# An attention, MLP and gated-convolution kernel: the residual u added by an accumulating store instead of by identity products

## The chip, the cores and the metric

The kernel runs on one core of a Trainium2 chip. The metric is the device time of one execution in microseconds; before the change three runs gave 1480.14, 1479.91 and 1478.4 us, median 1479.91.

The engines are named as in the profile: PE is TensorE (matmuls; PEld its weight loads), DVE is VectorE, ACT is ScalarE, POOL is GpSimd, and SP is SyncE, which issues DMAs.

## The reference

All arrays are float32. There are B = 8 batches of S = 576 tokens with D = 512 channels (8 heads of 64), so 4608 tokens.

```
scores = (q @ k.T) / 8, masked to block_i >= block_j (blocks of 64 tokens)
x  = softmax(scores) @ v                      # heads side by side: [8, 576, 512]
u  = x + (x.T @ U @ V).T                      # mixing over tokens, rank 32
z  = u + relu(u @ w_ch1) @ w_ch2              # MLP with 2048 hidden channels, residual u
gate = sigmoid(causal depthwise convolution of z, 5 taps)
out  = (gate * (z @ w_val)) @ w_out
```

The change concerns the line of z: how u is added to the MLP's result, and how the sum gets to DRAM, from where the gated stage reads it.

## The kernel before

Channels lie on partitions (four blocks d of 128), tokens along the free axis. The tokens of all batches form nine groups g of 512; a batch of 576 tokens is cut by the group boundaries into two pieces.

**Precision.** Every large product is made of three float32r products: each operand is split into a rounded part (names ending in h or hi) and the rest (l or lo), and hi·hi, hi·lo and lo·hi are added in PSUM. The rounded part is a copy on ACT (`hi_act`, L89), the rest a subtraction on POOL or DVE (`lo`, L95).

**Attention and mixing.** The attention of a pair of heads ends with x in a tile `xt` (five buffers), written by ACT out of PSUM (L605; the sums go to `lt`, L606) and multiplied on POOL by the reciprocal sums (L624). For the mixing it is transposed on PE (`mix_T`, L664, L672), multiplied with U (`mix_G`, L680), and in `mix_H` with V (L703); DVE adds the result into `xt` (L705), which then holds u, and ACT and POOL split it into the tiles uh and ul of its group. These tiles have two buffers, so pieces of a group that is too far ahead are put off (`later`) and done when the last step of an earlier group is out (`flush_later`); they come in a bunch around the change from one group to the next.

**The MLP.** For each group 16 steps f run over 128 hidden channels each. `emit_h1` makes 12 products (L833), ACT the rectified rounded part hh (L861) and DVE the rest hl (L862). `emit_o` makes 12 more with a block of W2 that SP loads from DRAM for each step into one of two buffers (L821), and adds them into four PSUM banks acc0 to acc3, one for each d (L885); for each d the order is hh, hl, hh. It runs one step behind `emit_h1`. In the first step of a group it first multiplies uh and ul with an identity matrix, for each d (L878): this puts u into acc. After the last step ACT copies acc to SBUF (L897), in tiles y with two buffers, and SP stores each of the four to `y_s` in DRAM (L898). Group 7's four copies go into tiles named gt, of which there are eight.

**Order of the work.** The order on PE is written out by hand: `gap()`, called twice in `emit_h1` and twice in `emit_o`, brings in the next pieces of the attention's stream at a fixed rate for each group. So around the change to a group PE runs: the last `emit_o` of the group before, `emit_h1` of steps 0 and 1 with pieces of attention between, then the first `emit_o`. All tiles of PSUM for attention and h come from four buffers with one tag. On the other engines and on SP a planner sets the order: it goes through the program with its own estimates of durations and gives each engine what is ready there by priority; the copies of acc, the tiles hh and hl and the additions into `xt` have a raised priority. Each engine then works through its list in that order, so an instruction that waits holds up everything behind it.

**After the MLP** (from 1268 us) `load_y` reads `y_s` back, DVE makes the gates, and PE the products with w_val (L975) and w_out (L999). The last group of `y_s` is read some rounds later than it is stored.

Of the kernel before, what the change touches and what calls it, by code (L numbers as in the profile page):

```python
# [9 lines left out]
F32R = mybir.dt.float32r  # L10
# [3 lines left out]
ALU = mybir.AluOpType  # L14
# [3 lines left out]
P = 128  # L18
# [4 lines left out]
def attn_moe_gate_kernel(ctx: ExitStack, tc: tile.TileContext, q, k, v, U, V, w1, w2, wval, convw, wout, out):  # L23
# [8 lines left out]
    ND = DM // P  # L32
    NF = DFF // P
# [52 lines left out]
    vec, act, pool, pe, sp = nc.vector, nc.scalar, nc.gpsimd, nc.tensor, nc.sync  # L86

    def hi_act(o, i):
        act.copy(o, i)  # L89
# [4 lines left out]
    def lo(eng, o, i, h):  # L94
        eng.tensor_tensor(o, i, f32(h), op=ALU.subtract)  # L95
# [51 lines left out]
    const = ctx.enter_context(tc.tile_pool(name="const", bufs=1, side="left"))  # L147
# [13 lines left out]
    def open_mlp_psum():  # L161
        first.close()
        psum["acc"] = mlp.enter_context(tc.tile_pool(name="accp", bufs=1, space=PSUM, side="left"))
# [38 lines left out]
    y_s = [dram.tile([P, ND, n], F32, name=f"y_s{g}") for g, (_, n) in enumerate(groups)]  # L202
# [15 lines left out]
    ident = ac_p.tile([P, P], F32, name="ident")  # L218
    make_identity(nc, ident)
    unit = const.tile([KC, KC], F32, name="unit")  # L220
    pool.tensor_copy(unit, ident[0:KC, 0:KC])
    identr = const.tile([P, P], F32R, name="identr")
    pool.tensor_copy(identr, ident)

    w1hi = w1_p.tile([P, ND, DFF], F32R, name="w1hi")
    w1lo = w1_p.tile([P, ND, DFF], F32R, name="w1lo")
# [400 lines left out]
    ut = {}  # L627
    gst = {}

    def u_tiles(g):  # L630
        if g not in ut:
            ut[g] = [u_p.tile([P, ND, GS], F32R, tag="u" + x, name="u" + x) for x in "hl"]
        return ut[g]


    def mix_pieces(b):
        t0, t1 = b * S, (b + 1) * S
        r = []
        for g, (a, n) in enumerate(groups):
            lo_t, hi_t = max(a, t0), min(a + n, t1)  # L640
            if lo_t < hi_t:
                r.append((g, lo_t - t0, hi_t - t0, lo_t - a))
        return r
# [3 lines left out]
    def mix_H2(pn):  # L647
        mix_H(pn, 0)
        yield
        mix_H(pn, 1)  # L650
# [39 lines left out]
    def mix_H(pn, i):  # L690
        pcs = mix_pieces(pn // NP)
        if i >= len(pcs):
            return
        gi, a0, a1, off = pcs[i]
        if gi >= 2 and gi > y_done[0] + 2:
            later.append((pn, i))
            return
        xt = xts[pn]
        d = pn % NP
        uh, ul = u_tiles(gi)  # L700
        w = a1 - a0
        ps = ps_p.tile([P, 512], F32, tag="a", name="pH")
        pe.matmul(ps[:, 0:w], gst[pn], vst[:, a0:a1], start=True, stop=True)  # L703
        with tc.high_priority():
            vec.tensor_tensor(xt[:, a0:a1], ps[:, 0:w], xt[:, a0:a1], op=ALU.add)  # L705
        hi_act(uh[:, d, off:off + w], xt[:, a0:a1])
        lo(pool, ul[:, d, off:off + w], xt[:, a0:a1], uh[:, d, off:off + w])

    def flush_later():
        if later and mix_pieces(later[0][0] // NP)[later[0][1]][0] <= y_done[0] + 2:  # L710
            mix_H(*later.pop(0))
# [113 lines left out]
    accs = {}  # L825
# [43 lines left out]
    def emit_o(s, gap):  # L869
        g, f = divmod(s, NF)  # L870
        t0, n = groups[g]
        if f == 0:
            if g == 0:
                open_mlp_psum()
            accs[g] = [psum["acc"].tile([P, GS], F32, tag=f"acc{d}", name=f"acc{d}") for d in range(ND)]
            for d in range(ND):
                for i, u in enumerate(ut[g]):
                    pe.matmul(accs[g][d][:, 0:n], identr, u[:, d, 0:n], start=(i == 0), stop=False)  # L878
        acc = accs[g]
        hh, hl = hts.pop(s)  # L880
        w = w2t.pop(s)
        for d in range(ND):
            ds = slice(d * P, (d + 1) * P)
            for i, (wi, x) in enumerate(((0, hh), (0, hl), (1, hh))):
                pe.matmul(acc[d][:, 0:n], w[:, wi, ds], x[:, 0:n], start=False, stop=(f == NF - 1 and i == 2))  # L885
            if d == 1:
                gap()
        gap()
        if f == NF - 1:
            ut.pop(g)  # L890
            for d in range(ND):
                if pbp and g < NG - 1:
                    y = pbp["g"].tile([P, GS + HALO], F32, tag="gt", name="gt")
                else:
                    y = late["y"].tile([P, GS], F32, tag="y", name="y")
                with tc.high_priority():
                    act.copy(y[:, 0:n], acc[d][:, 0:n])  # L897
                sp.dma_start(out=y_s[g][:, d, :], in_=y[:, 0:n])  # L898


    wv = {}
# [156 lines left out]
    def gap():  # L1058
        tick_count[0] += 1
        if tick_count[0] % EVERY == 0:  # L1060
            flush_later()
        pace[0] += pace[1]
        while pace[0] > 0 and pace[2] == 0:
            pace[0] -= 1.0
            r = next(stream, 2)
            if r:
                pace[2] = r
                if r == 2:
                    while later:
                        flush_later()  # L1070
                    open_pb()

    gated_conv[0] = GATE0
    for s in range(NS + LAG):
        g, f = divmod(s, NF)
# [5 lines left out]
        if f == 0 and g < B:  # L1081
            while g > 0 and not pace[2]:
                pace[0] = 1.0
                gap()
            if g > 0:
                emit_o(s - LAG, gap)
            if pace[2] != 2:
                pace[2] = 0
            aim(g)
        if s < NS:  # L1090
# [11 lines left out]
            if g == NG - 1 and 4 <= f < 4 + 2 * ND:  # L1102
                g_, d = divmod(f - 4, ND)
# [3 lines left out]
        if s >= LAG and not (f == 0 and g < B):  # L1107
            emit_o(s - LAG, gap)
# [54 lines left out]
```

## Time and profile before

| | |
|---|---|
| runs | 1480.14, 1479.91, 1478.4 us; median 1479.91 |
| profiled execution | span 1473.3 us; what lies around the span is the 6.6 us to the median of the runs |
| PE | 1426.3 us busy (97%), 6706 matmuls |
| DVE | 1054.8 us (72%) |
| ACT | 718.5 us (49%) |
| POOL | 297.8 us (20%) |
| DMA | 163.56 MB, all on SP's queue but for instructions |
| chain that ended last | PE 82%, DVE 10%, DMA 3%; line L878 in it 1% |

The span runs from the first to the last instruction; the profiled execution has no time of its own beside it, so its time is taken as span plus 6.6 us. A row of a timeline gives start, duration, engine, line, operation, tiles and shapes, the number of instructions merged into it, and in brackets the idle time before it with what ended it. Rows of a list of waits give the total in us, the number of waits and the longest. Matmuls overlap: their durations are longer than the distance between their starts.

### The profile page before, as it was taken

The page shows a single profiled execution, that of the slowest core. Times are in us where ns is not written, and L with a number is a line of the kernel's source. Part 1 is how long each engine was busy: PE and PEld are TensorE (multiplying, and loading weights), DVE is VectorE, ACT ScalarE, POOL GpSimd, SP SyncE. Part 2 cuts the span into 40 slices and gives each one's busy share as a digit, 9 for nine tenths or more (in the row PEclk, how much of TensorE's full clock was granted, in tenths as well). Part 3 has the DMA queues.
Part 4 walks back from the last instruction along what each step waited for, and adds up shares of the span by engine and source line. Part 5 has one row for each costly group of instructions (what it writes and reads, how often), then busy time and mean ns, then how long its engine had stood idle before and what let it go on. Part 6 is the DMA issues. An engine that isn't in the chain of part 4 may idle for free.

```text
span 1473.3 us, 20082 instructions
## 1 busy us (share of the span) xinstructions
PE 1426.3 (97%) x6706; PEld 1102.3 (75%) x6706; DVE 1054.8 (72%) x2224; ACT 718.5 (49%) x1529; POOL 297.8 (20%) x420
## 2 busy tenths in 40 slices
PE   6888899899999999999999999999999999999999
PEld 3656666677777777777777777777888888788887
DVE  7878877967786888777778878777224326399991
ACT  4676564555555546565555555555322221344332
POOL 2113332212121112112211211121122100343310
PEclk9999999999999999999999999999999999999999
DMA  6445764543343434333434433332255433223311
GB/s 123 104 106 154 217 210 130 152 110 96 84 102 110 95 96 111 96 86 82 124 82 111 114 83 96 96 95 70 86 159 167 147 128 123 92 72 101 109 56 65
DMA packets 246288, 163.56 MB, mean 111 GB/s; under 512 B 197669, under 2 KB 212261, under 8 KB 246186
## 3 DMA queue, kind: packets, MB, share of 16 engines
q1 hardware_dynamic: 246186, 162.29, 39.6%
q8 instruction: 53, 0.87, 0.3%
q14 instruction: 49, 0.40, 0.1%
HBM read 134.98 MB, written 27.26 MB: 110 GB/s over the span
## 4 chain that ended last, share of the span: by engine, by line
PE 82%; DVE 10%; DMA 3%; ACT 2%; issue 1%; SPq 1%; POOL 0%; DVEq 0%; ACTq 0%
PE acc L885 25%; PE h L833 25%; PE pPV L604 8%; PE o L999 7%; PE val L975 6%; PE pS L381 6%; DMA raw<-in_moe_w_ch_dram 1%; DVE wa L123 1%; DVE rq L425 1%; PE pG L680 1%; PE acc L878 1%; PE pS L416 1%; DVE wa L141 1%; PE pT L664 1%; DVE wa L120 1%
## 5 line engine op out<-in xcount | busy, mean ns | idle before, releaser
L885 PE MATMUL acc<-hh,w 128*128 128x512 f32 x1152 | 401.0, 402 | 0.0
L885 PEld LDWEIGHTS acc<-hh,w 128*128 128x128 f32 x1152 | 217.1, 188 | 67.6 <-issue 22.5
L833 PE MATMUL h<-uh,w1hi 128*128 128x512 f32 x576 | 238.5, 414 | 2.3 <-ACT lt L606 1.2
L833 PE MATMUL h<-uh,w1lo 128*128 128x512 f32 x576 | 226.4, 393 | 0.0
L885 PE MATMUL acc<-hl,w 128*128 128x512 f32 x576 | 225.9, 392 | 0.0
L833 PE MATMUL h<-ul,w1hi 128*128 128x512 f32 x576 | 225.7, 392 | 0.0
L862 DVE SCALAR_TENSOR_TENSOR hl<-h,hh 128x512 fp32r<-128x512 f32 x144 | 98.5, 684 | 143.2 <-ACT hh L861 142.0
L861 ACT ACTIVATE hh<-h 128x512 fp32r<-128x512 f32 x144 | 85.9, 596 | 173.9 <-PE h L833 167.9
L833 PEld LDWEIGHTS h<-uh,w1hi 128*128 128x128 f32 x576 | 108.6, 189 | 45.7 <-issue 20.4
L95 POOL TENSOR_TENSOR vlo<-vstk,vhi 128x320 fp32r<-128x320 f32 x46 | 43.0, 934 | 455.3 <-ACT vhi L89 389.2
L833 PEld LDWEIGHTS h<-uh,w1lo 128*128 128x128 f32 x576 | 108.4, 188 | 24.2
L885 PEld LDWEIGHTS acc<-hl,w 128*128 128x128 f32 x576 | 108.8, 189 | 19.8 <-issue 0.7
L833 PEld LDWEIGHTS h<-ul,w1hi 128*128 128x128 f32 x576 | 108.7, 189 | 19.6 <-issue 1.3
L957 DVE SCALAR_TENSOR_TENSOR gt<-yb,cw,gt 128x516 f32<-128x516 f32 (+1 forms) x144 | 115.2, 830 | 1.4
L381 PE MATMUL pS<-tq,tk 64*128 64x320 f32 (+4 forms) x576 | 96.7, 429 | 1.5 <-DVE hl L862 0.8
L95 POOL TENSOR_TENSOR yl<-yb,yh 128x512 fp32r<-128x512 f32 (+7 forms) x64 | 66.9, 1078 | 107.4 <-ACT yh L89 107.3
L386 ACT COPY s<-pS 128x320 f32<-128x320 f32 (+2 forms) x128 | 60.2, 497 | 48.7 <-PE pS L381 47.5
L95 POOL TENSOR_TENSOR ul<-xt,uh 128x512 fp32r<-128x512 f32 (+7 forms) x64 | 53.8, 850 | 108.0 <-ACT uh L89 107.9
L536 ACT ACTIVATE s<-s 128x448 f32<-128x448 f32 (+1 forms) x62 | 44.0, 710 | 64.8 <-DVE s L512 64.8
L381 PEld LDWEIGHTS pS<-tq,tk 64*128 64x128 f32 x576 | 43.8, 185 | 37.8 <-issue 22.2
L512 DVE TENSOR_TENSOR s<-s,mb 128x64 f32<-128x64 f32 (+4 forms) x160 | 68.7, 493 | 0.3
L605 ACT COPY xt<-pPV 64x128 f32<-64x128 f32 (+1 forms) x128 | 50.1, 391 | 25.8 <-PE pPV L604 23.9
(169 smaller groups left out, 2758.8 us busy)
## 6 DMA issues: line engine op xcount, KB each, us to landing
w<-w_s SPq DMA_DIRECT2D x144, 512.0 KB, 3.3
rawq<-in_q_dram SPq DMA_DIRECT2D x128, 72.0 KB, 2.8
rawk<-in_k_dram SPq DMA_DIRECT2D x128, 72.0 KB, 3.1
out_dram<-ot SPq DMA_DIRECT2D x35, 256.0 KB, 2.0
vstk<-in_v_dram SPq DMA_DIRECT2D x64, 128.0 KB, 2.7
raw<-in_moe_w_ch_dram SPq DMA_DIRECT2D x64, 128.0 KB, 2.8
raw<-in_moe_w_ch_dram SPq DMA_DIRECT2D x16, 512.0 KB, 3.9
w_s<-wo SPq DMA_DIRECT2D x16, 512.0 KB, 3.3
```

The lines of the kernel that those rows point to most:

```text
L95: eng.tensor_tensor(o, i, f32(h), op=ALU.subtract)
L381: pe.matmul(t[:, o:o + w], tk[me, kslice(j)], tq[me, a0:a1], start=True, stop=True)
L386: act.copy(stt[n][half_of[j]][:, d:d + o], t[:, 0:o])
L512: noted(3, vec.tensor_tensor(sv(n, j), sv(n, j), mb[:, q0[j]:], op=ALU.subtract))
L604: pe.matmul(o_, l_, r_, start=(i == 0), stop=(i == len(todo) - 1))
L833: pe.matmul(ps[:, 0:n], w[:, d, fs], x[:, d, 0:n], start=(d == 0 and i == 0), stop=(d == ND - 1 and i == 2))
L861: act.activation(hh[:, 0:n], ps[:, 0:n], AF.Relu)
L862: latest[0] = vec.scalar_tensor_tensor(hl[:, 0:n], ps[:, 0:n], 0.0, f32(hh[:, 0:n]), op0=ALU.max, op1=ALU.subtract)
L885: pe.matmul(acc[d][:, 0:n], w[:, wi, ds], x[:, 0:n], start=False, stop=(f == NF - 1 and i == 2))
L957: vec.scalar_tensor_tensor(gt[d][:, 0:gw], y[:, d, j:j + gw], cw[:, d, j:j + 1], gt[d][:, 0:gw], op0=ALU.mult, op1=ALU.add)
L975: pe.matmul(ps[:, 0:n], w[:, d, es], x[:, d, 0:n], start=(i == 0), stop=(i == 3 * ND - 1))
L999: pe.matmul(ps[:m, cs], x[:, e, a:a + m], w[:, e, cs], start=(i == 0), stop=(i == 3 * ND - 1))
```

## The change

`mix_H` gets a DMA from SP that writes each piece of u, as soon as it stands in `xt`, to the place in `y_s` where the MLP's result will go. The identity products are gone, and the first product with W2 of a group starts the accumulation in PSUM. The stores of the MLP's result are issued by POOL instead of SP, as DMAs that add to what lies in DRAM. The identity matrix in float32r isn't made any more.

```diff
@@ -219,8 +219,6 @@
     pool.tensor_copy(unit, ident[0:KC, 0:KC])
-    identr = const.tile([P, P], F32R, name="identr")
-    pool.tensor_copy(identr, ident)
@@ -703,6 +701,7 @@
         with tc.high_priority():
             vec.tensor_tensor(xt[:, a0:a1], ps[:, 0:w], xt[:, a0:a1], op=ALU.add)
+        sp.dma_start(out=y_s[gi][:, d, off:off + w], in_=xt[:, a0:a1])
         hi_act(uh[:, d, off:off + w], xt[:, a0:a1])
@@ -873,16 +872,13 @@
             accs[g] = [psum["acc"].tile([P, GS], F32, tag=f"acc{d}", name=f"acc{d}") for d in range(ND)]
-            for d in range(ND):
-                for i, u in enumerate(ut[g]):
-                    pe.matmul(accs[g][d][:, 0:n], identr, u[:, d, 0:n], start=(i == 0), stop=False)
         acc = accs[g]
...
             for i, (wi, x) in enumerate(((0, hh), (0, hl), (1, hh))):
-                pe.matmul(acc[d][:, 0:n], w[:, wi, ds], x[:, 0:n], start=False, stop=(f == NF - 1 and i == 2))
+                pe.matmul(acc[d][:, 0:n], w[:, wi, ds], x[:, 0:n], start=(f == 0 and i == 0), stop=(f == NF - 1 and i == 2))
@@ -895,7 +891,7 @@
                 with tc.high_priority():
                     act.copy(y[:, 0:n], acc[d][:, 0:n])
-                sp.dma_start(out=y_s[g][:, d, :], in_=y[:, 0:n])
+                pool.dma_start(out=y_s[g][:, d, :], in_=y[:, 0:n], accum_op=ALU.add)
```

## Rows read from the trace of the kernel before

**Rows 1.** Stretches: length, each engine's busy us (instructions), granted clock, DMA share, GB/s.

```profile
140.00:306.00 166.00, 152.35 (x684) 109.69 (x685) 135.76 (x280) 90.89 (x193) 47.45 (x53) 0.97 0.59 172
...
575.00:708.00 133.00, 133.00 (x658) 102.41 (x657) 104.67 (x233) 73.58 (x157) 24.31 (x44) 1.00 0.38 99
```

**Rows 2.** Waits of ACT: total us, times, longest us.

```profile
ACT y L897 <- DMA y_s<-y: 17.2, 9, 3.5
```

**Rows 3.** The identity products, line L878: durations in ns, first and last start.

```profile
L878 PE MATMUL acc<-uh,identr x36: 387/389/475, 140.1 to 1186.9; 128*128 128x512 f32 x36
...
L878 PE MATMUL acc<-ul,identr x36: 389/389/397, 140.4 to 1187.1; 128*128 128x512 f32 x36
```

**Rows 4.** Timeline of PE: first product with W2 of group 3.

```profile
586.83 0.39 PE L885 MATMUL acc<-hh,w 128*128 128x512 f32 x1
```

**Rows 5.** Timeline of PE: the second identity product of groups 1 to 7.

```profile
318.30 0.39 PE L878 MATMUL acc<-ul,identr 128*128 128x512 f32 x1
...
452.06 0.39 PE L878 MATMUL acc<-ul,identr 128*128 128x512 f32 x1
...
585.24 0.39 PE L878 MATMUL acc<-ul,identr 128*128 128x512 f32 x1
...
718.30 0.39 PE L878 MATMUL acc<-ul,identr 128*128 128x512 f32 x1
...
851.62 0.39 PE L878 MATMUL acc<-ul,identr 128*128 128x512 f32 x1
...
984.66 0.39 PE L878 MATMUL acc<-ul,identr 128*128 128x512 f32 x1
...
1096.35 0.39 PE L878 MATMUL acc<-ul,identr 128*128 128x512 f32 x1
```

**Rows 6.** Timeline of DVE: hl of the first step of groups 1 to 8.

```profile
318.25 0.69 DVE L862 SCALAR_TENSOR_TENSOR hl<-h,hh 128x512 fp32r<-128x512 f32 x1 [0.37 <-ACT hh L861]
...
452.32 0.65 DVE L862 SCALAR_TENSOR_TENSOR hl<-h,hh 128x512 fp32r<-128x512 f32 x1
...
585.30 0.67 DVE L862 SCALAR_TENSOR_TENSOR hl<-h,hh 128x512 fp32r<-128x512 f32 x1
...
719.57 0.65 DVE L862 SCALAR_TENSOR_TENSOR hl<-h,hh 128x512 fp32r<-128x512 f32 x1
...
851.85 0.67 DVE L862 SCALAR_TENSOR_TENSOR hl<-h,hh 128x512 fp32r<-128x512 f32 x1
...
985.58 0.67 DVE L862 SCALAR_TENSOR_TENSOR hl<-h,hh 128x512 fp32r<-128x512 f32 x1
...
1094.77 0.69 DVE L862 SCALAR_TENSOR_TENSOR hl<-h,hh 128x512 fp32r<-128x512 f32 x1 [3.23 <-ACT hh L861]
...
1180.93 0.69 DVE L862 SCALAR_TENSOR_TENSOR hl<-h,hh 128x512 fp32r<-128x512 f32 x1 [4.75 <-ACT hh L861]
```

**Rows 7.** Timeline of ACT around the change to group 3.

```profile
574.63 0.59 ACT L897 COPY y<-acc 128x512 f32<-128x512 f32 x1 [1.78 <-PE acc L885]
...
578.77 0.58 ACT L897 COPY y<-acc 128x512 f32<-128x512 f32 x1 [2.63 <-DMA y_s<-y]
...
584.29 0.60 ACT L861 ACTIVATE hh<-h 128x512 fp32r<-128x512 f32 x1
```

**Rows 8.** DMA issues by line: queue, count, KB each, median us to landing.

```profile
w<-w_s SPq DMA_DIRECT2D x144, 512.0 KB, 3.3
...
y_s<-y SPq DMA_DIRECT2D x32, 256.0 KB, 2.9
...
yb<-y_s SPq DMA_DIRECT2D x2, 256.0 KB, 4.2
```

**Rows 9.** SP's issues of y (ns min/median/max), and POOL's timeline in the change to group 7.

```profile
L898 SPq DMA_DIRECT2D y_s<-y x32: 319/320/637, 307.4 to 1272.0; - x32
...
1093.82 1.29 POOL L95 TENSOR_TENSOR ul<-xt,uh 128x512 fp32r<-128x512 f32 x1 [2.80 <-ACT uh L89]
```

## The prediction

> **What bounds the kernel now.** I read the table of stretches first. From 306 us on TensorE (PE) is busy practically all the time: 133.00 of 133 us in one group's stretch, against 104.67 for VectorE (DVE), 73.58 for ScalarE (ACT) and 24.31 for GpSimd (POOL); the granted clock is 1.00, the upper level of 2.4 GHz. Only before 306 us do others set the pace: between 140 and 306 us PE has 152.35 of 166 us [rows 1]. So matmuls that disappear after 306 us shorten the program, unless what comes after them isn't ready. That is the question here, and the timelines around the nine group changes answer it.
>
> A second reading, of the waits: nine times ACT stood before a y copy until a store of y had landed, 17.2 us in all, up to 3.5 [rows 2]. Tag y has two buffers, so the third copy of a group waits for the first store.
>
> **Identity products.** There are 36+36 of them, and each lasts 389 ns by its row [rows 3]; but matmuls overlap, and what counts is the distance between starts. In the change from group 2 to 3 the second one starts at 585.24 and the first product with W2 at 586.83 [rows 4, 5]: seven distances of 0.227 us, so eight are 1.82 us, and nine groups 16.4 us. That is the most the change can bring (72 x 0.389 = 28.0 us would be the wrong sum).
>
> **What they cover.** Without them the first W2 product moves to where the first identity product was. It needs hh, and the one after it, at the place of the second identity product, needs hl of the same step. I compare the start of that second identity product [rows 5] with the end of hl [rows 6], by the group that begins:
> - group 1: 318.30, hl ends 318.94: late by 0.64
> - group 2: 452.06, 452.97: 0.91
> - group 3: 585.24, 585.97: 0.73
> - group 4: 718.30, 720.22: 1.92
> - group 5: 851.62, 852.52: 0.90
> - group 6: 984.66, 986.25: 1.59
> - group 7: 1096.35, 1095.46: early by 0.89
> - group 8: hl ends 1181.62, and the last product of that burst starts at 1187.1 [rows 3], so the burst itself at 1185.5: no wait.
>
> So in groups 1 to 6 the products hide a late hl, and PE keeps only the rest of 1.82: 1.18, 0.91, 1.09, 0, 0.92, 0.23, together 4.33 us. Groups 7 and 8 keep 1.82 each. Group 0 lies at 140 us, where PE has waits for ACT and DVE left in which its 1.82 can vanish; I take 0 there (at most 1.82). With everything else unchanged: 4.33 + 3.64 = 8.0 us.
>
> Why hl is late: ACT. In the change to group 3 it copies y at 574.63, must wait for a landing until 578.77, and hh of the new group comes only at 584.29 [rows 7], behind an unbroken row of copies and exponentials that all queued up meanwhile. What delays the third y copy delays hh, hl and PE one for one.
>
> **The new store.** Call d the extra time from y copy to landing with POOL's accumulating DMA instead of SP's plain one. In groups 1 to 6 d is lost in full on PE; in group 7 what exceeds 0.89. Group 8's copies lie at the end of the MLP; what ACT does late there are casts for the products with w_out, which come only after all four products with w_val, so I cost it at nothing. In the change into group 8 the y of group 7 goes through four free gt buffers and waits for nothing. So for d over 0.89 the gain is 4.33 - 6d + (1.82 + 0.89 - d) + 1.82 = 8.86 - 7d, and the balance is at d = 1.27.
>
> No row shows a DMA issued by POOL or one that accumulates. Bounds: below, 0, the landing of 2.9 us that SP's store has today for 256 KB; above, if the old contents must be read first as in a load of 256 KB of y_s (4.2 us) and the issue takes POOL 1.29 as its longest tile operation here does, against SP's 0.32: d = 4.2 + 0.97 = 5.2 [rows 8, 9]. I take 1.1, near the lower end, because bytes are cheap in these rows: 512 KB of w land in 3.3, 0.4 more than 256 KB of y, which stands for the additional read, and POOL's issue at about 1.0 adds 0.7. Gain: 8.86 - 7.7 = 1.2 us.
>
> The Trainium skill ("DMA: Bandwidth & Descriptors", section "Anatomy of one DMA — SWDGE (gpsimd) path") gives 2.0 us plus the bytes over 436 GB/s for a DMA from GpSimd, as an estimate 2.6 us for 256 KB: less than SP's 2.9 here, and by it d would be 0 and the gain 8.0. The same page ("Rules for kernel authors") says that an accumulating DMA reads its destination and writes it later, which speaks against that price; no run here shows either.
>
> **The rest of the edit.** 64 stores of u on SP (one for each addition into xt) at 0.32 us, less 36 of y: 9 us more issue time on a queue that mostly waits for free weight buffers. Between the release of a w buffer and the use of what is loaded into it lie three blocks of twelve products, 36 x 0.227 = 8.2 us, and the load lands in 3.3 [rows 8]: a short delay on SP costs nothing. If that cover went, PE would wait for w, which it does nowhere now. The store also holds xt some 3 us longer; a group's stretch of 133 us holds some four pairs of heads, 33 us each, and there are five buffers: nothing. The stores add 9.4 MB, the accumulation reads another 9.4, beside a DMA share of 0.38 (0.59 before 306 us) [rows 1]: nothing by itself. On POOL the four DMAs wait for ACT's copies, and ul, vlo and the softmax corners queue behind them. POOL is idle 2.80 us before even the ul of the fullest pieces [rows 9], and that ul is for a group later. It costs nothing, as long as the planner doesn't place a DMA ahead of work that is ready. The cast of identr falls away at the start, beside loads: nothing.
>
> Sum: the profiled span 1473.3 becomes 1472.1. The median of the three runs lies 6.6 above the span (1479.9), so 1478.7.
>
> **Rivals.**
> A (forecast): most of the gain goes to late hl and a somewhat slower store, d between 0.5 and 2.3 around my 1.1. That reaches from 1474.9 to 1487.2 (gain 4.97 to -7.2), with no change to be seen for d from 0.84 to 1.7.
>
> B: faster. Either the DMA is about as quick as SP's (d under 0.5), or the planner, which orders ACT by its own estimate of landings, puts the copies of the PV results ahead of y copies three and four, so that the landing blocks nothing. For it: ACT has nothing else to do in its 2.63 us before the third copy [rows 7], so little needs to move. Against: an order moves only if the planner thinks the new DMA late. d = 0 gives 1471.9; with group 0's part and hl no longer late the limit is 1479.9 - 16.4 = 1463.5.
>
> C: slower. The accumulating DMA reads before it writes and POOL's issue is long, d over 2.3. Place: ACT before the third y copy, at the changes into groups 1 to 7. It decides from d = 1.7 on, where 8.86 - 7d passes -3. d = 3 is -12.1 us, 1492.0; the bound of 5.2 would give -27.5, 1507. For it: ACT already waits there, and reads of y_s land later than those of w though they are half the size [rows 8]. Against: in the rows of w and y more bytes cost little.
>
> D: hidden anyway: DVE and ACT, not PE, limit the attention part, and even B's gain vanishes in later waits of PE: 1479 to 1480. Against: DVE has 28 of 133 us free [rows 1].
>
> **Chances.** A 0.45, B 0.25, C 0.26, D 0.04. Runs of this kernel can't tell less than 0.2% (3 us) from no change. Of A I put 0.10 below d = 0.84, 0.25 in the middle and 0.10 above 1.7. So faster is 0.35 (B and A's lower end), same 0.29 (A's middle and D), slower 0.36. The range reaches upward to d = 2.8 (1490.6), and downward to B with d = 0 and group 0's part (1470.1): 1470 to 1491, which leaves out the rest of B and C, some 0.2.
>
> **What would show it.** Right: no L878 rows; at each change into groups 1 to 6 PE waits about 0.6 to 2 us plus d for hl at L885; ACT's waits for y_s grow from 17.2 us to about 25. B is right if ACT's waits for y_s shrink or lie behind the PV copies, and PE has no new wait at L885 beyond those listed. C is right if the waits for y_s exceed 3.5 + 1.7 us each. Wrong altogether: new PE waits inside a group (w, xt, or POOL's corners), or a DVE that shows up before PE over whole stretches.

## The result, and the profile after

The changed kernel is slower: 1493.45 us, median of four runs (1492.13 to 1494.95), against 1479.16 for four of the kernel before (1474.22 to 1480.14). The ratio is 1.0103, with an interval of 1.0079 to 1.0127. My forecast of 1478.7 was wrong, and so was the upper end of the range, 1491. The place named in rival C is where the time goes.

The stretch of one group, which answers to [rows 1] (columns as there):

```profile
575.00:708.00 133.00, 130.97 (x640) 99.98 (x639) 102.70 (x230) 73.13 (x156) 25.07 (x46) 0.99 0.44 104
```

PE was busy 133.00 of 133 us and now stands still for 2 of them; the clock is 0.99 instead of 1.00.

ACT's wait for a store of y, which answers to [rows 2] (total us, times, longest):

```profile
ACT y L893 <- DMA y_s<-y: 30.8, 10, 5.2
```

PE's waits from 300 us on, in the same columns:

```profile
PE pT L670 <- ACT lt L604: 12.4, 6, 3.1
PE acc L881 <- ACT hh L860: 4.0, 5, 2.2
PE h L832 <- DVE hl L861: 2.4, 1, 2.4
PE val L971 <- DVE gf L975: 2.2, 1, 2.2
PE acc L881 <- DVE hl L861: 2.2, 3, 1.2
```

The same view of the kernel before has only 1.7 us there:

```profile
PE pT L672 <- ACT lt L606: 0.9, 2, 0.7
PE val L975 <- DVE gf L979: 0.8, 1, 0.8
```

So 17.2 us of ACT's waiting became 30.8, and 1.7 us of PE's became 23.2. The chain from the one to the other is seen in ACT's timeline at the change into group 3, as in [rows 7]:

```profile
575.29 0.59 ACT L893 COPY y<-acc 128x512 f32<-128x512 f32 x1 [1.79 <-PE acc L881]
...
583.13 0.59 ACT L893 COPY y<-acc 128x512 f32<-128x512 f32 x1 [3.66 <-DMA y_s<-y]
...
585.77 0.53 ACT L604 COPY lt<-pPV 64x448 f32<-64x448 f32 x1
...
587.16 0.59 ACT L893 COPY y<-acc 128x512 f32<-128x512 f32 x1
587.64 0.60 ACT L860 ACTIVATE hh<-h 128x512 fp32r<-128x512 f32 x1
```

The first y copy ends at 575.88; its tile is free again for the third copy at 583.13, 7.25 us later. In [rows 7] it was 578.77 − 575.22 = 3.55. Behind the third copy in ACT's list stand the copy of the softmax sums into `lt` and, further on, hh of the new group, which starts 12.35 us after the first y copy instead of 9.66. PE needs `lt` first. Its timeline answers to [rows 4, 5]; the first product with W2 is now the first in its bank:

```profile
586.35 0.30 PE L670 MATMUL pT<-ident,xt 128*64 128x128 f32 x1 [2.03 <-ACT lt L604]
...
588.49 0.63 PE L881 MATMUL acc<-hh,w 128*128 128x512 f32 x1
```

The change into group 4 has the longest of these waits, and shows what follows it:

```profile
722.68 0.30 PE L670 MATMUL pT<-ident,xt 128*64 128x128 f32 x1 [3.14 <-ACT lt L604]
...
723.28 0.39 PE L832 MATMUL h<-uh,w1lo 128*128 128x512 f32 x1
723.51 0.48 PE L832 MATMUL h<-uh,w1hi 128*128 128x512 f32 x1
723.79 0.63 PE L832 MATMUL h<-ul,w1hi 128*128 128x512 f32 x1
724.21 0.63 PE L832 MATMUL h<-uh,w1lo 128*128 128x512 f32 x1
```

At first the products start 0.23 us after one another, and then 0.42: the clock has gone from its level of 2.4 GHz to 1.2. Stretches of 10 us at or behind group changes, the first at full clock and the others low (the third number from the end is the granted clock):

```profile
450.00:460.00 10.00, 7.78 (x33) 5.91 (x34) 6.01 (x14) 5.47 (x11) 1.70 (x2) 1.00 0.49 106
580.00:590.00 10.00, 7.97 (x34) 5.86 (x33) 8.06 (x20) 6.83 (x14) 2.60 (x3) 0.86 0.83 153
720.00:730.00 10.00, 6.81 (x17) 4.67 (x18) 6.87 (x15) 7.80 (x16) 2.62 (x3) 0.68 0.46 57
860.00:870.00 10.00, 9.86 (x40) 8.17 (x41) 5.50 (x14) 6.26 (x14) 1.74 (x2) 0.83 0.53 103
1110.00:1120.00 10.00, 7.56 (x21) 5.59 (x21) 3.27 (x7) 1.72 (x3) 2.34 (x4) 0.69 0.93 236
```

With the stretches at 310 and 1300 (0.87 each) and those just below 1, the shortfall (10 us x (1 − clock), over all stretches from 300 us on) adds up to 13.6 us. The kernel before has 0.0 by the same sum up to 1470 us. The first stretch stands behind a wait of 2.14 us for `lt`, so not every wait of that length is followed by a low clock.

**The account.** From the first y copy of group 0 to the end of the span the kernel before took 1166.5 us and the changed one 1189.3: 22.8 more. It is made of −14.6 (eight groups' identity products at 1.82), +21.5 (PE's waits, 23.2 less 1.7), +13.6 (clock), and 2.3 that I can't place. The part ahead of that copy was 3.8 us shorter; over all kernels here that part varies between 299.2 and 310.3 us with hardly a difference in its code, so I don't credit the change with it. Together: 19.0 from span to span (1473.3 to 1492.3), 4.7 more than between the medians, because the profiled execution before was a quick one of its kernel.

The store of y among the DMAs by line, which answers to [rows 8], and then the issues of the stores of y and of u, for [rows 9] (columns as there):

```profile
y_s<-y POOLq DMA_DIRECT2D x32, 256.0 KB, 5.8
```

```profile
L894 POOL DMA_DIRECT2D y_s<-y x32: 806/875/1195, 303.9 to 1296.2; - x32
...
L704 SPq DMA_DIRECT2D y_s<-xt x64: 319/442/2007, 65.7 to 1102.6; - x64
```

A store that landed in 2.9 us now takes 5.8, and the stores of u stand in SP's list with 0.44 us each.

### The profile page after: what moved, and what is told of

It is laid out like the page before. It is cut to its first block, busy times and chain, and to the rows that moved or that the text cites. A ratio compares the mean times of both kernels' runs of the same rounds, so it can differ in the third digit from the quotient of the medians.

```text
span 1492.3 us, 20082 instructions
## 1 busy us (share of the span) xinstructions
PE 1423.5 (95%) x6634; PEld 1094.8 (73%) x6634; DVE 1058.0 (71%) x2224; ACT 717.7 (48%) x1529; POOL 325.6 (22%) x455
## 3 DMA queue, kind: packets, MB, share of 16 engines
HBM read 134.98 MB, written 36.70 MB: 115 GB/s over the span
## 4 chain that ended last, share of the span: by engine, by line
PE 79%; DVE 9%; DMA 5%; ACT 3%; issue 2%; POOL 1%; SPq 1%; ACTq 0%; DVEq 0%; POOLq 0%
PE acc L881 24%; PE h L832 23%; PE pPV L602 8%; PE o L995 7%; PE val L971 6%; PE pS L379 5%; DMA raw<-in_moe_w_ch_dram 2%; DMA y_s<-y 2%; PE pS L414 1%; PE pG L678 1%; PE pE L454 1%; DMA y_s<-xt 1%; PE pT L662 1%; DVE wa L123 1%; DVE s L510 1%
## 5 line engine op out<-in xcount | busy, mean ns | idle before, releaser
L881 PE MATMUL acc<-hh,w 128*128 128x512 f32 x1152 | 407.0, 407 | 4.0 <-ACT hh L860 4.0
L881 PEld LDWEIGHTS acc<-hh,w 128*128 128x128 f32 x1152 | 220.7, 192 | 75.1 <-issue 23.4
L881 PE MATMUL acc<-hl,w 128*128 128x512 f32 x576 | 229.3, 398 | 2.2 <-DVE hl L861 2.2
L881 PEld LDWEIGHTS acc<-hl,w 128*128 128x128 f32 x576 | 110.7, 192 | 24.2 <-DVE hl L861 4.6
L95 POOL TENSOR_TENSOR ul<-xt,uh 128x512 fp32r<-128x512 f32 (+7 forms) x64 | 57.0, 902 | 96.2 <-ACT uh L89 96.1
```

The costliest lines, as they stand in the source:

```text
L881: pe.matmul(acc[d][:, 0:n], w[:, wi, ds], x[:, 0:n], start=(f == 0 and i == 0), stop=(f == NF - 1 and i == 2))
```

## The experiments

Three things changed at once (SP to POOL, plain to accumulating, 64 stores of u), and the loss could lie in any of them; or it could lie in what stands behind the copy on ACT, whatever the store costs. Each ratio is against runs of the kernel before taken beside it on the same chip. The theories in the expectations are T1, the round trip of the store through ACT; T2, the missing cover of hl; and T3, the stores of u. The measure for the turnaround is the time from the end of a group's first y copy to the start of its third, mean over the changes into groups 1 to 7: 3.74 us before, 7.36 after.

**Which part of the store is slow?** e1 takes SP and a plain store, e2 POOL and a plain store; both keep the stores of u, which are overwritten, so the result lacks u.

```diff
-                pool.dma_start(out=y_s[g][:, d, :], in_=y[:, 0:n], accum_op=ALU.add)
+                sp.dma_start(out=y_s[g][:, d, :], in_=y[:, 0:n])      # e1
+                pool.dma_start(out=y_s[g][:, d, :], in_=y[:, 0:n])    # e2
```

> The changed kernel with one edit: the MLP's result is stored by SP with a plain DMA (so u is written, then overwritten: the result lacks u). Theory T1, the round trip: POOL's accumulating DMA lands 3 to 4 us later than SP's plain one, and the third y copy, ACT and then PE wait for it. T1 expects what the prediction gave for d = 0: 5 to 8 us under before, 1471 to 1474 us, ACT's waits for y_s near 17 us in total, PE waits of 0.6 to 2 us for hl at L881. T2, the missing cover: without the identity products PE meets a late hl whatever the store, and its clock falls after the wait; expects 1479 or more and low clock at the group changes. T3, the stores of u: 64 more DMAs in bunches at the group changes slow all that lands there; expects 1486 or more, and y's landing over 4 us.

> The changed kernel with the store of y still issued by POOL, but plain, without accumulation (the result lacks u). It splits d into issue and accumulation. T1 with the accumulation as the price: landing near 3.5 us, 1473 to 1478 us. T1 with POOL's descriptor work as the price: landing near 5.8 us as in the changed kernel, 1488 to 1494 us. T3 (stores of u): like the changed kernel, 1488 to 1494 us.

e1: 1475.44, ratio 0.9995 (0.9981 to 1.0009). e2: 1479.34, 1.0007 (0.9992 to 1.0022). Both are far from the changed kernel's 1.0103, so accumulation, not the issue from POOL, parts them. But e1 did not become faster, though it has SP's plain store of before and no identity products. Its waits of PE:

```profile
PE pT L670 <- ACT lt L604: 8.0, 6, 1.7
```

and its store in SP's list and the third copy on ACT, at the change into group 3 (first copy at 575.56, ended 576.15):

```profile
576.82 0.44 SPq L704 DMA_DIRECT2D y_s<-xt  x1
577.36 0.88 SPq L894 DMA_DIRECT2D y_s<-y  x2
```

```profile
582.32 0.59 ACT L893 COPY y<-acc 128x512 f32<-128x512 f32 x1 [2.57 <-DMA y_s<-y]
```

Over all 32 stores the landing from issue is a median of 2.8 us, as before. But the store that counts is the first of a group: it is issued 0.7 us after its copy in the mean of the seven changes instead of 0.03 (1.2 here, behind a load of k and a store of u) and lands 4.8 us after its issue instead of 3.6. The turnaround is 5.62 (6.17 in this change). In e2 it is 5.40, with a median landing of 4.1:

```profile
y_s<-y POOLq DMA_DIRECT2D x32, 256.0 KB, 4.1
```

So e1's turnaround is 1.9 us longer than before with neither accumulation nor POOL, and moving the plain store to POOL adds nothing to it. What the two kernels have beyond the kernel before are the stores of u at the group change, and what they lack are the identity products; e6 tells which it is.

**The stores of u moved away from the group change.** e6 keeps the accumulating store, but drops the store of u in `mix_H` and writes as many bytes from hh in the middle of the group (u isn't in the result). In the trace they begin 49 to 76 us behind the first y copy of a group change.

```diff
-        sp.dma_start(out=y_s[gi][:, d, off:off + w], in_=xt[:, a0:a1])
...
+        if f == 8:
+            for d in range(ND):
+                sp.dma_start(out=y_s[g][:, d, :], in_=f32(hh)[:, 0:n])
```

> The changed kernel with the 64 stores of u at the group changes replaced by four plain stores of 256 KB in the middle of each group (of hh of step 8, so the result holds that instead of u); the accumulating stores stay. It tells whether the bunch of u stores is what makes the accumulating store land in 5.8 us and more. T3: landing falls to 4 us or less, and the time to 1475 to 1481. T1 (the accumulation itself is slow): landing stays at 5.5 us or more, time 1487 to 1494.

1479.61, ratio 1.0020 (1.0003 to 1.0037). The turnaround falls from 7.36 to 5.44, the landing to 5.2:

```profile
y_s<-y POOLq DMA_DIRECT2D x32, 256.0 KB, 5.2
```

but PE still waits:

```profile
PE pT L670 <- ACT lt L604: 10.2, 6, 2.1
```

With e2 the two parts of the turnaround can be told apart: the u stores at the change bring 7.36 − 5.44 = 1.9 us, accumulation 7.36 − 5.40 = 2.0; and the kernel before, with neither, has 3.74. The landing stayed above the 4 us that T3 had expected, and the time came out where T3 had put it: either part taken away alone brings the kernel back to within 0.2% of the kernel before.

**A third buffer for y.** It takes the wait away from the third copy.

```diff
-        late["y"] = lpool("yp", 2)
+        late["y"] = lpool("yp", 3)     # e3; e4: the same in the kernel before, with a buffer of r1 less
```

> The changed kernel with three buffers for y instead of two. T1: the third copy waits for nothing and the fourth was placed 4 us later already, so ACT's waits for y_s fall from 31 to under 8 us, the PE waits for ACT lt at L670 (12.4 us) go nearly all, and the time falls to 1466 to 1476 us, faster than before. T2: PE still waits for hl and its clock falls; 1484 us or more. T3: 1488 us or more.

> The kernel before with three buffers for y (a buffer of r1 less, to make room). It shows what the third buffer is worth without the change, since there the identity products cover ACT's lateness and PE waits for ACT only 0.9 us at L672. T1: 1477 to 1480 us, no change, though ACT's waits for y_s fall from 17 to under 5 us. T2 and T3 expect the same; if it gains as much as e3 does over the changed kernel, the buffer helps by another way than T1's.

e3: 1483.91, 1.0042 (1.0025 to 1.0059). e4: 1475.14, 0.9983 (0.9970 to 0.9996). T1 had expected 1466 to 1476 us of e3, and that is not what happened: the wait went to the fourth copy (first the store, then the waits; the profiled execution, 1478.61 us, is the quickest of e3's eight):

```profile
y_s<-y POOLq DMA_DIRECT2D x32, 256.0 KB, 8.0
```

```profile
ACT y L893 <- DMA y_s<-y: 27.2, 8, 5.4
...
PE pT L670 <- ACT lt L604: 12.6, 6, 2.7
```

With three stores in flight the median landing rises to 8.0 us. A buffer helps by 0.6%; PE's waits for `lt` are as long as in the changed kernel. For the kernel before it is worth 0.17%.

**An attempt at the order that did nothing.** Copies three and four were put behind `emit_h1` in the program and lost their raised priority, in the changed kernel (e5), the kernel before (e7) and e1 (e8).

```diff
-            for d in range(ND):
+            def put(d):
...
-                with tc.high_priority():
+                with tc.high_priority() if d < 2 or pbp else nullcontext():
...
+            for d in range(ND):
+                if d < 2 or pbp:
+                    put(d)
+                else:
+                    behind_h1.append((put, d))
...
             emit_h1(s, gap)
+            while behind_h1:
+                put, d = behind_h1.pop(0)
+                put(d)
```

> The changed kernel, but the copies of acc2 and acc3 of a group are emitted behind the next group's first emit_h1, without raised priority, so that ACT does PV copies and exponentials first and doesn't stand before a y buffer that is still being stored. T1 (round trip of the accumulating store through ACT): the PE waits for ACT lt at L670 (12.4 us in the changed kernel) nearly vanish, what is left is some wait for hl, and the clock stays up: 1468 to 1477 us. T2 (missing cover): hl is late whatever ACT does; 1483 or more. T3 (stores of u slow what lands at the changes): no gain over the changed kernel, 1488 or more.

> The kernel before with the same late copies of acc2 and acc3 as in e5. T1: PE hardly waits for ACT there (0.9 us), so no change beyond 0.3%: 1473 to 1479 us, though ACT's waits for y_s (17.2 us) go down to under 5. T2 and T3 expect the same.

> The changed kernel with SP's plain store (the result lacks u) and the late copies of e5: the identity products gone, no accumulation and ACT not blocked. It is what the removal of the products is worth when nothing takes its place. T1: 16.4 us less what hl is still late, 1462 to 1470 us. T2: PE still waits for hl by 0.6 to 2 us at six changes, so 1469 to 1475 us, hardly under e1 (1475.4). T3: about e1.

Ratios 1.0102 (1.0081 to 1.0123), 0.9991 (0.9979 to 1.0003) and 0.9998 (0.9984 to 1.0012): each is where its kernel was. The planner left ACT's order as it was: the y copies, the copies of the PV results and hh follow one another at all seven changes in e5 as in the changed kernel, in e7 as in the kernel before and in e8 as in e1, and e5's six waits at `lt` add up to 13.5 us where the changed kernel has 12.4. So these three are repeats, no test of the order.

**The order forced.** Now the planner is told that copies three and four come after hh of the next group's first step, so nothing that PE waits for stands behind them. e9 is the changed kernel, e10 is e1, e11 the kernel before, e12 is e6, each so.

```diff
+            hh_at[0] = act.activation(hh[:, 0:n], ps[:, 0:n], AF.Relu)
...
-                with tc.high_priority():
+                with tc.high_priority() if d < 2 or pbp else tc.issue_after(hh_at[0].ins):
```

> The changed kernel with the third and fourth copy of acc put into ACT's order behind hh of the next group's first step (the late copies of e5 had left ACT's order as it was). By then the first two accumulating stores have had some 8 us, so ACT waits for y_s under 5 us in all. T1 (the turnaround blocks ACT): PE's waits for ACT lt at L670 vanish, 1467 to 1476 us. T2 (missing cover): PE waits for hl stay, 1480 or more. T3 (the u stores fill SP's queue and delay the rest): some gain, since the accumulation is no longer waited for, but SP's list stays long: 1478 to 1486 us.

> The changed kernel with SP's plain store of y (the result lacks u) and the same forced order. What the removal of the products is worth when neither accumulation nor ACT's wait is in the way. T1: 16.4 us less a few tenths per change: 1460 to 1467 us. T2: 1471 to 1477 us. T3: between, 1466 to 1472.

> The kernel before with the same forced order. T1: there the products cover ACT's lateness and PE waits for ACT 0.9 us in all, so 1474 to 1478 us, no change. If the order itself is worth something without the change, it would show here as more than 0.2%.

> The accumulating stores with the u stores moved to the middle of each group (four plain stores of hh of step 8 instead of u, as in e6) and the forced order. T1: about e9, 1465 to 1475 us. T3: clearly under e9, by 5 us or more. T2: 1478 or more.

e9: 1480.23, 1.0021 (1.0004 to 1.0038). e10: 1465.92, 0.9930 (0.9912 to 0.9948). e11: 1472.82, 0.9973 (0.9963 to 0.9984). e12: 1474.28, 0.9983 (0.9968 to 0.9997). ACT at the change into group 3 in e10:

```profile
568.64 0.59 ACT L894 COPY y<-acc 128x512 f32<-128x512 f32 x1 [1.79 <-PE acc L882]
...
575.55 0.53 ACT L604 COPY lt<-pPV 64x448 f32<-64x448 f32 x1
...
576.94 0.60 ACT L861 ACTIVATE hh<-h 128x512 fp32r<-128x512 f32 x1
577.44 0.58 ACT L894 COPY y<-acc 128x512 f32<-128x512 f32 x1
```

The third copy stands behind hh and waits for nothing. In e9 and e10 the six waits for `lt` are gone, and with them the waits of more than 2 us; what is left is above all the late hl (e9 first, then e10):

```profile
PE acc L882 <- DVE hl L862: 8.9, 6, 1.9
```

```profile
PE acc L882 <- DVE hl L862: 6.9, 6, 1.7
```

ACT's waits for the store are down to 8.4 us in e9, and it is 0.8% faster than the changed kernel for the order alone; e12 against e9 shows that u's stores at the group change still cost 0.4% then. T1 alone had expected 1467 to 1476 us of e9: the order takes away what T1 names, and what is left, the late hl and the stores of u, is T2's and T3's. The order is worth something in the kernel before too, 0.3% (e11), where T1 had expected nothing; so against e11, which has the same order, e9 is still 0.5% slower. e10 also measures the removal of the identity products by itself, u's stores included: against e11, 1465.92 − 1472.82 = −6.9 us, which the intervals leave open by some 3 us either way. Its six waits of 1.04, 1.23, 0.50, 1.70, 0.87 and 1.53 us are the late hl of my list, which had 6.69 in sum. The clock's shortfall is 0.1 us in e10 and 5.2 in e9.

**The products with hl last.** The cover that the identity products gave can be had without them: in a group's first step all eight products with hh go first, the four with hl last. e13 does that to the changed kernel, e14 adds the forced order.

```diff
+        first_step = [(d, i) for i in (0, 2) for d in range(ND)] + [(d, 1) for d in range(ND)]
+        steps = first_step if f == 0 else [(d, i) for d in range(ND) for i in range(3)]
```

> The changed kernel with one edit: in the first step of a group the four hl products go behind the eight hh products, so that eight products cover a late hl as the identity products did. T1 (the turnaround of the store is the cause): ACT is late by its wait for y, PE still waits at L670, and only the waits for hl at L881 (2.2 us and part of the rest) go: 1487 to 1494 us. T2 (the missing cover is the cause): 6 to 10 us faster than the changed kernel, 1482 to 1487.

> e9 (accumulating stores, third and fourth copy behind hh) with the hl products last. With ACT free and hl covered, the accumulation is waited for only at the change into group 7 and at the end of the MLP. T1 and T2 together: e9 less its waits for hl (about 10 us) and the clock they cost: 1468 to 1474 us. If the u stores or the accumulation slow the rest by another way: 1475 or more.

e13: 1490.3, 1.0071 (1.0048 to 1.0093). e14: 1468.03, 0.9927 (0.9912 to 0.9942), with the whole computation and the accumulating store. The waits of PE in e13, then in e14:

```profile
PE pT L670 <- ACT lt L604: 13.9, 6, 3.2
PE acc L884 <- ACT hh L860: 3.8, 4, 2.5
```

```profile
PE acc L885 <- ACT y L897: 4.2, 3, 2.2
PE acc L885 <- ACT hh L861: 1.7, 2, 1.0
```

The four cells of the two edits on the changed kernel: neither 1.0103, cover alone 1.0071, order alone 1.0021, both 0.9927. Each lateness hid the other: the cover is worth 0.3% while PE waits for `lt`, which the overlapping intervals hardly tell from nothing, and 0.9% once it doesn't. Against e11, which has the order without the change, e14 is 0.5% faster: that is what the change gives when both latenesses are dealt with.

**A better version.** e15 writes u to a DRAM tensor of its own, stores y plainly from SP in the forced order, and lets POOL add u to `y_s` by two DMAs from DRAM to DRAM, for which neither PE, ACT nor DVE waits in the attention part. The program has them in step 8 of the next group, but in the trace POOL issues each about as soon as it can after its two stores of y: at the change into group 3 in e16 at 578.88 and 588.24, the first store of y being issued at 572.53. e16 adds hl last.

```diff
+        sp.dma_start(out=u_s[gi][:, d, off:off + w], in_=xt[:, a0:a1])
...
+    def add_u(g):
+        for h in (0, 2):
+            pool.dma_start(out=y_s[g][:, h:h + 2, :], in_=u_s[g][:, h:h + 2, :], accum_op=ALU.add)
...
+        if f == 8 and g > 0:
+            add_u(g - 1)
```

> u is stored to a tensor of its own, y plainly by SP with the forced order of e10, and at step 8 of the next group POOL issues two DMAs that add u to y in DRAM; the output is complete. If the accumulation costs only whom it makes wait: as e10, 1464 to 1469 us. If it takes something by itself (DMA engines, POOL): 1472 or more.

> e15 with the hl products of the first step last. PE's waits for hl in e10 add up to 6.9 us over six changes; they should go: 1457 to 1463 us, under every kernel so far. If PE meets another wait at once: 1463 to 1467.

e15: 1473.35, 0.9958 (0.9943 to 0.9974). e16: 1463.27, 0.9895 (0.9870 to 0.9920): the whole computation, faster than the kernel before and than the changed one, and 0.8% faster than e11. e15 is 0.3% slower than e10, so of its two expectations the second came true, by which the addition takes something by itself. Beside it SP's plain stores of y land in a median of 5.2 us (e15 and e16) instead of 2.8 (e10). PE's waits in e16 and the stretch of group 3:

```profile
PE acc L892 <- DMA w<-w_s: 2.8, 2, 1.5
PE val L990 <- DVE gf L994: 0.8, 1, 0.8
```

```profile
575.00:708.00 133.00, 133.00 (x661) 102.53 (x659) 106.49 (x238) 74.65 (x160) 25.77 (x46) 1.00 0.51 119
```

PE is busy all of it again, at full clock. The 2.8 us for w are new, two waits at the change into group 7: the loads of w issued at 1089.56 and 1097.26 land 9.5 and 8.8 us later, and POOL issues additions at 1084.87 and 1094.68, which land after 8.3 and 9.4. In e10, without them, the loads of w at this change, issued at 1091.90 and 1097.34, land after 7.9 and 4.9 us and PE doesn't wait.

## Why the prediction was wrong

**The identity products' worth** (1.82 us a group, 8.0 in all with the store unchanged): right as far as it could be measured. e10 against e11 gives 6.9 us, give or take 3, with u's stores included and the order forced in both. With the planner's own order e1, the case of d = 0, gained only 2.0, because the stores of u lengthened the turnaround.

**The late hl**: right in place, and with the order forced in size, 6.9 us in six waits in e10 against 6.69. In the changed kernel it is hardly seen (2.2 us in three waits), because PE is held up earlier.

**The new store, d**: here it failed. I took 1.1 us for the extra time from copy to landing; the turnaround grew from 3.74 to 7.36, d = 3.62. It was inside the bounds of 0 and 5.2, and I took a value near the lower one with the argument that bytes are cheap. Two terms make up d: accumulation, 2.0 us (e2), and the stores of u next to it, 1.9 us (e6). The first I had at 0.4 for the additional read; the second I had costed at nothing, in the sentence on DMA share: the mean share over 133 us hides that the stores come in a bunch just when y is stored (at the change into group 3 five of them are issued from 571.33 to 576.56, and the first store of y at 576.17). That d came out nearer the upper bound doesn't make the load of 4.2 us the right guide, since that bound had nothing for u. The move of the issue to POOL, for which I had 0.7, adds nothing: e2's turnaround is 0.2 us shorter than e1's, and the ratios differ by 0.0012, within their intervals.

The Trainium skill ("DMA: Bandwidth & Descriptors", "Anatomy of one DMA — SWDGE (gpsimd) path") gave an estimate of 2.6 us for this store. The trace has 4.1 without accumulation (e2) and 5.8 with it, both beside other traffic; the measurement decides. The rule of the Trainium skill on the same page ("Rules for kernel authors") that an accumulating DMA reads its destination and writes it later fits the difference of 1.7, which doesn't prove that this is its cause.

**Where PE would lose it**: the mechanism was right (rival C: ACT stands before the third y copy at each change into groups 1 to 7), though not by the mark that I had set for it: C's waits were each to exceed 5.2 us, and six of them are 2.3 to 4.8 and one, the change into group 7, 5.18. The place on PE was half right. I expected hl at L881; the first thing that is late is `lt` at L670, because its copy stands between the third y copy and hh on ACT. I had looked only at hh behind the copy, not at each instruction between.

**The formula** 8.86 − 7d gives −16.5 with d = 3.62, close to the 14.3 us between the medians, but by two errors that cancel. ACT's lateness isn't lost one for one: by the formula PE would have waited for 6.69 + 7 x 3.62 − 0.89 = 31.1 us, and waited 21.5 more than before. And the clock's 13.6 us were in no term. Over the kernels the shortfall goes with the longer waits of PE rather than with their sum: 13.6 and 10.2 us where waits reach 3.1 and 3.2 (after, e13), 5.2 where the longest is 1.9 (e9), and up to 1460 us none in e1, e10 and e16, where no wait is over 1.7 (e1 has 8.0 us of waits at `lt`). But e12, whose longest is 1.9 as in e9, has none up to there either, so what sets it no run isolates.

**Rival B** happened in part: at each change into groups 1 to 6 the planner put the first pair of PV copies ahead of the third y copy, and the second pair, for which PE waits, ahead of the fourth but behind the third, where the kernel before has all four y copies first; e9 shows what the full movement is worth, 0.8% on the changed kernel.

**Group 8, at nothing**: wrong, but small. At the end of the MLP POOL issues its DMAs behind a subtraction of the next stage, and ACT's third and fourth copies wait:

```profile
1280.23 5.81 POOL L95 TENSOR_TENSOR yl<-yb,yh 128x64 fp32r<-128x64 f32 x8 [39.24 <-ACT yh L89]
1285.98 1.71 POOL L894 DMA_DIRECT2D y_s<-y  x2
```

```profile
1292.03 0.59 ACT L893 COPY y<-acc 128x512 f32<-128x512 f32 x1 [0.35 <-DMA y_s<-y]
1295.33 0.59 ACT L893 COPY y<-acc 128x512 f32<-128x512 f32 x1 [2.72 <-DMA y_s<-y]
```

PE's wait at w_val is 2.2 us instead of 0.8, and the clock is low behind it (0.87 at 1300). Here a queue that the store was moved to did have work ahead of it.

**The time around the span**: I took 6.6 us. The profiled execution after took 1494.02 with a span of 1492.3, so it is 1.7; the profiled execution before, 1473.3 in span, was a quick one of its kernel and not the median.

**Open**: why u's stores slow POOL's queue as much as SP's no run tells. Of the accumulating store the pages of the profile show where a part of its time lies. For the same bytes the packets on POOL's queue took more than twice the share of the 16 DMA engines' time (the changed kernel first, then e2; packets, MB, share):

```profile
q0 software_dynamic: 5184, 9.44, 4.6%
```

```profile
q0 software_dynamic: 2880, 9.44, 1.8%
```

So the packets themselves take longer, and there are more of them. Whether that is a reading of the destination stays open: the page's count of bytes read from HBM is 134.98 MB in both.

## What to carry to other kernels

Before a store is made slower, list what stands behind the next copy into its buffer on the copying engine: everything in that list waits with the copy for the store. Price DMAs by what else is in flight at that moment, not by the mean share of a long stretch. And when two latenesses lie on one another, taking one away shows little; change the order and the cover together before you drop either.

## What the runs showed of the hardware

- An accumulating store of 256 KB from POOL lands in 5.2 to 6.5 us at the median with two buffers (e6, after, e14) and in 8.0 with three (e3); plain from POOL in 4.1 (e2). Its issue takes POOL 0.875 us, that of a plain one 0.557.
- From DRAM to DRAM, 512 KB are added in 7.8 us (e16):

```profile
y_s<-u_s POOLq DMA_DIRECT2D x18, 512.0 KB, 7.8
```

- TensorE's clock after short waits: behind waits of 2.03, 3.14 and 2.36 us (groups 3 to 5) and 2.44 us (group 7) the granted clock of the stretches shown above was 0.86, 0.68, 0.83 and 0.69; behind 2.14 us (group 2) it stayed at 1.00. By the sum above the low clock cost the changed kernel more than half as much again as the waits themselves. Behind six waits of 0.5 to 1.7 us, one at each change, e10 has no such stretch. e9 has 0.83 behind waits of 1.00 and 1.53 us and 0.75 behind 1.94, but 1.00 behind single waits of 1.84 and 1.88; and e12 has 1.00 behind the same pair of waits, 0.99 and 1.53. So the length of the waits doesn't decide it.
